# Dilated sliding attention and a two-layer network: q and k turned on VectorE in 32x32 squares, scores summed over two halves of d, loads cut and ordered anew

## The chip, the cores and the metric

The kernel runs on one NeuronCore of one Trainium2 chip. Five engines work on it side by side, each through its own instructions in their order: TensorE (PE in the profile; its weight loads are PEld), VectorE (DVE), ScalarE (ACT), GpSimd (POOL) and SyncE (SP). Transfers between memory and the core's SBUF are issued here by POOL (all loads, which also turn f32 into f16 on the way) and by SP (all stores). The metric is device time in microseconds, from the first instruction to the last of one execution and what lies around it. Three runs of the kernel before gave 331.77, 331.92 and 332.44 us.

## The reference

The inputs q, k and v are 8 batches x 8 heads x 576 positions x 64 (d), all f32. Heads 0 to 3 are plain, heads 4 to 7 are strided.

```
scores = q @ k.T / 8
plain:   key j counts for query i where 0 <= i - j < 32
strided: key j counts for query i where 0 <= i - j < 128 and (i - j) % 4 == 0
attn   = softmax over the keys that count
x      = attn @ v, heads side by side: 4608 tokens x 512
out    = silu(x @ w_in) @ w_out        w_in 512 x 2048, w_out 2048 x 512
```

## The kernel before, in words

**Attention.** In the code `z` is 0 for plain and 1 for strided heads, `b` is the batch. The 576 positions of a plain head are 18 blocks of 32 queries (`QB`), and a block sees 64 keys (`KB`): its own 32 and the 32 ahead. A strided head falls into four classes of 144 positions (position modulo 4), each of which is a plain problem of five blocks, the last half empty. Four heads lie at once on the 128 partitions of a score tile, 32 queries each.

For q and k, d has to lie on the partitions. `load_qk` (line 88) brings several positions of two heads to a partition, as f16, into a tile `n` of the pool `nat` (two buffers). `transpose` (199) turns them on PE against an identity matrix into PSUM tiles `t` of the pool `ps` (four buffers, one bank each), and VectorE and ScalarE copy those into `qT`, `kT` (plain) and `qC`, `kC` (strided), half each (`copies`). `score` (257) and `score_class` (269) are one matmul each for a head and a block: 64 rows (d), 32 columns (queries), 64 keys. `scores` (334) issues 72 of them for a batch's plain heads and 80 for its strided ones, and then on VectorE scales and masks them (`masked`, 288) and takes the maxima (`reduce_max`). `exps` (380) runs on ScalarE, a block at a time with a sum, or, where `shift` (370) has subtracted the maximum on VectorE, in one instruction. `normal` (398) divides on VectorE, and `turned` (413) turns the result, f16, in squares of 32x32 with VectorE's own transpose. `values` (456) multiplies with v on PE, and `finish` (472) casts the result into `xT` on VectorE: the plain heads side by side (478), the strided ones with each element four positions on (480).

**The two layers.** `layer1` (513) runs 16 steps `f`, each eight matmuls of 128x128 weights and 288 tokens into a tile of the pool `big` (two buffers of two banks) and one silu on ScalarE into `gT`. `layer2` (566) serves two batches in nine tiles of 128 tokens, four behind the even and five behind the odd batch: 16 matmuls of 512 columns into a buffer of `big`, a copy `ob` on VectorE, a store. Batch 0 is cut into tokens 0 to 255 and 256 to 575, so that its first layer can start on the first part (`layer1_part`, 530), and its four output tiles are summed side by side (`layer2_first`, 546).

**Order.** The order on each engine is the order in which the program issues its work. From batch 0 on, `plan_of` (601) gives the attention of later batches its place: `plan(s)` issues what is set for step `s`, steps 0 to 15 ahead of the `f` of layer one and steps 16 on ahead of every fourth matmul of layer two. In batch 0, steps -16 to -1 belong to its first part. `later` places `normal`, `turned`, `values` and `finish` of a softmax. Each engine waits at an instruction until its inputs and its buffer are ready, and what is queued behind it waits too. The loads all stand on POOL, in the order of lines 156 to 170, 690 to 700 and the plan.

Of the kernel before, what the change touches and what calls it, by code (L numbers as in the profile page):

```python
# [14 lines left out]
P = 128  # L15
W = 32
# [5 lines left out]
HF = P // 2  # L22
UR = 4
URS = (9, 12)
# [3 lines left out]
def kernel(  # L28
# [13 lines left out]
    HP = H // 2  # L42
    HH = H // 2
# [3 lines left out]
    NM = NB // 2  # L47
    CL = S // DIL
    UPS = [S // u for u in URS]
# [3 lines left out]
    PA = SA // UR  # L53
    PB = (S - SA) // UR
# [16 lines left out]
    ident = cpool.tile([P, P], F16, name="ident")  # L71
# [7 lines left out]

    kTs = [cpool.tile([P, HP // 2, W + S], F16, name=f"kT{i}") for i in range(2)]  # L80
    qTs = [cpool.tile([P, HP // 2, S], F16, name=f"qT{i}") for i in range(2)]
    kCs = [cpool.tile([P, HH, 2, W + CL + TL], F16, name=f"kC{i}") for i in range(2)]
    qCs = [cpool.tile([P, HH, 2, CL + TL], F16, name=f"qC{i}") for i in range(2)]

    NC = CL // W + 1
    vws = [cpool.tile([P, NB + NC * DIL, D], F16, name=f"vw{i}") for i in range(2)]

    def load_qk(b):

        for which in (0, 1):  # L90
            t = nat.tile([P, 2 * sum(URS), D], F16, tag=f"n{which}", name=f"n{which}_{b}")
            u0, u1 = 2 * URS[0], 2 * (URS[0] + URS[1])
            qk[b, 0, which] = t[:, 0:u0].rearrange("p (h u) d -> p h u d", h=2)
            qk[b, 1, which] = t[:, u0:u1].rearrange("p (h u) d -> p h u d", h=2)
        for z in (1, 0) if b == 1 else (0, 1):
            for which, src in ((1, k), (0, q)):
                for i in (0, 1):
                    h = 2 * (2 * z + i)
                    nc.gpsimd.dma_start(  # L99
                        out=qk[b, z, which][i * HF : i * HF + UPS[z]].rearrange("p h u d -> p h (u d)"),  # L100
                        in_=src[b, h : h + 2].rearrange("h (p u) d -> p h (u d)", u=URS[z]),
                    )

    def load_qk0(part, kinds):

        t0, n = ((0, PA), (SA, PB))[part]
        if part not in qk0:
            tiles = [nat.tile([P, 2 * sum(URS), D], F16, tag=f"n{w}", name=f"n{w}_0{part}") for w in (0, 1)]
            qk0[part] = [t[:, 0 : H * UR].rearrange("p (h u) d -> p h u d", h=H) for t in tiles]
        for h in kinds:  # L110
# [6 lines left out]
    def load_v(b, strided=(0, NC), plain=(0, NB)):  # L117
# [12 lines left out]
        for h in range(HH if plain[0] < plain[1] else 0):  # L130
# [3 lines left out]
            )  # L134

    qk = {}
    qk0 = {}
    FC = DFF // 4

    def load_w_in(c):  # L140
# [550 lines left out]
    for c in (1, 2, 3):  # L691
        load_w_in(c)
# [70 lines left out]
```

## Time and profile before

| | |
|---|---|
| median of three runs | 331.92 us (331.77 to 332.44) |
| the profiled execution | 332.05 us, of which 330.3 us are its span |
| mean granted clock of TensorE | 0.984 |
| PE busy | 304.7 us, 92% of the span |
| VectorE busy | 199.3 us, 60% |
| ScalarE busy | 212.5 us, 64% |
| GpSimd busy | 104.3 us, 32% |
| matmuls of layers one and two (lines 518, 537, 578, 554) | 116.4, 20.1, 114.6 and 15.7 us busy |
| transposes of q and k on PE (215, 243, 251) | 11.5, 2.6 and 2.5 us busy |
| loads of k and q in batches 1 to 7 | 56 issues of 144 KB, 5.7 and 6.0 us to landing |
| loads of v | 100 issues of 8 to 72 KB |

A group of the profile names the line, the engine, the operation and the tiles (output before the arrow, inputs behind it), how often it ran, the busy time, and the mean time of one. Matmuls overlap in the array, so that their mean times are longer than the time from one start to the next. The chain that ended last is a list of pieces of work, each released by the one before it; it shows where time was spent that nothing else could cover. The windows give the busy time of each engine within a stretch of the span, with the clock that TensorE was granted.

### The profile page before, as it was taken

The page shows a single profiled execution, that of the slowest core. Times are in us where ns is not written, and L with a number is a line of the kernel's source. Part 1 is how long each engine was busy: PE and PEld are TensorE (multiplying, and loading weights), DVE is VectorE, ACT ScalarE, POOL GpSimd, SP SyncE. Part 2 cuts the span into 40 slices and gives each one's busy share as a digit, 9 for nine tenths or more (in the row PEclk, how much of TensorE's full clock was granted, in tenths as well). Part 3 has the DMA queues.
Part 4 walks back from the last instruction along what each step waited for, and adds up shares of the span by engine and source line. Part 5 has one row for each costly group of instructions (what it writes and reads, how often), then busy time and mean ns, then how long its engine had stood idle before and what let it go on. Part 6 is the DMA issues. An engine that isn't in the chain of part 4 may idle for free.

```text
span 330.3 us, 11556 instructions
## 1 busy us (share of the span) xinstructions
PE 304.7 (92%) x5032; PEld 195.1 (59%) x5032; DVE 199.3 (60%) x369; ACT 212.5 (64%) x703; POOL 104.3 (32%) x178
## 2 busy tenths in 40 slices
PE   3476999479999999999999999999999999999995
PEld 2445764147754577547764577457754677467644
DVE  5578289761679975587558555787558534550011
ACT  2675673306599866997599556996699466916300
POOL 8583728759600291039101940043000000000000
PEclk9997999979999999999999999999999999999999
DMA  6999999999942298029702990049002100110022
GB/s 82 134 101 203 197 192 90 188 220 82 99 78 77 58 127 122 34 69 130 119 4 79 123 175 6 34 79 94 4 20 79 65 2 2 66 64 2 2 83 76
DMA packets 56098, 28.58 MB, mean 87 GB/s; under 512 B 34032, under 2 KB 51568, under 8 KB 56048
## 3 DMA queue, kind: packets, MB, share of 16 engines
q0 software_dynamic: 50720, 18.41, 46.9%
q1 hardware_dynamic: 5328, 9.44, 7.9%
q8 instruction: 39, 0.64, 0.8%
q14 instruction: 11, 0.09, 0.1%
HBM read 36.70 MB, written 9.44 MB: 140 GB/s over the span
## 4 chain that ended last, share of the span: by engine, by line
PE 76%; DVE 9%; ACT 7%; DMA 4%; issue 2%; POOL 1%; POOLq 0%; DVEq 0%; ACTq 0%
PE h L518 34%; PE o L578 29%; ACT pe L393 4%; PE h L537 3%; PE x L446 3%; PE t L215 3%; DMA n<-in_q_dram 3%; DVE pn L409 2%; DMA out_dram<-ob 2%; DVE pt L421 2%; PE s L273 1%; DVE ms L290 1%; DVE nm L328 1%; PE s L261 1%; DVE ob L563 1%
## 5 line engine op out<-in xcount | busy, mean ns | idle before, releaser
L526 ACT ACTIVATE gT<-h 128x576 f16<-128x576 f32 x112 | 72.8, 650 | 70.8 <-PE h L518 70.0
L518 PE MATMUL h<-xT,w_in 128*128 128x288 f16 x896 | 116.4, 288 | 1.9 <-DVE xT L478 1.9
L578 PE MATMUL o<-w_out,gT 128*128 128x512 f16 (+1 forms) x528 | 114.6, 373 | 0.0
L518 PEld LDWEIGHTS <-w_in 128*128 128x128 f16 x896 | 86.4, 98 | 26.4 <-issue 2.5
L393 ACT ACTIVATE pe<-ms,nm 128x64 f32<-128x64 f32 x256 | 85.0, 334 | 5.7 <-DVE nm L328 5.6
L578 PEld LDWEIGHTS <-gT 128*128 128x128 f16 x528 | 50.2, 98 | 54.5
L563 DVE COPY ob<-o 128x512 f32<-128x512 f32 (+1 forms) x37 | 24.7, 669 | 46.4 <-PE o L578 44.0
L121 POOL DMA_DIRECT2D vw<-in_v_dram x32 | 22.0, 693 | 93.4 <-PE x L446 91.2
L393 ACT ACTIVATION_READ_ACCUMULATOR pe<-ms,nm 128x1 f32 x256 | 48.1, 188 | 0.0
L290 DVE SCALAR_TENSOR_TENSOR ms<-s,mask 128x512 f32<-128x512 f32 (+2 forms) x33 | 22.3, 680 | 41.5 <-PE s L273 23.7
L421 DVE STREAM_TRANSPOSE pt<-pn 128x640 f16<-128x640 f16 (+2 forms) x32 | 26.0, 812 | 1.1
L409 DVE TENSOR_TENSOR pn<-pe,r 128x640 f16<-128x640 f32 (+2 forms) x32 | 25.3, 792 | 1.1
L328 DVE TENSOR_REDUCE nm<-ms 128x10 f32<-128x640 f32 (+2 forms) x32 | 25.2, 786 | 1.1
L131 POOL DMA_DIRECT2D vw<-in_v_dram x36 | 23.4, 663 | 4.6 <-DMA vw<-in_v_dram 3.0
L537 PE MATMUL h<-xT,w_in 128*128 128x256 f16 (+1 forms) x128 | 20.1, 318 | 4.0 <-ACT gT L544 3.5
L554 PE MATMUL o<-w_out,gT 128*128 128x512 f16 x64 | 15.7, 399 | 4.3 <-DVE ob L563 4.3
L480 DVE CAST xT<-x 128x288 f16<-128x288 f32 x28 | 19.0, 824 | 0.0
L537 PEld LDWEIGHTS <-w_in 128*128 128x128 f16 x128 | 13.5, 108 | 9.3 <-DMA w_in<-in_moe_w_in_dram 3.8
L126 POOL DMA_DIRECT2D vw<-in_v_dram x32 | 15.9, 513 | 9.3 <-DMA w_out<-in_moe_w_out_dram 7.9
L99 POOL DMA_DIRECT2D n<-in_q_dram x28 | 16.5, 612 | 5.8 <-DMA w_in<-in_moe_w_in_dram 4.0
L99 POOL DMA_DIRECT2D n<-in_k_dram x28 | 16.8, 618 | 4.7 <-PE t L215 2.4
L446 PEld LDWEIGHTS <-vw 32*64 32x64 f16 (+1 forms) x1264 | 13.3, 110 | 7.9 <-issue 7.9
(62 smaller groups left out, 214.6 us busy)
## 6 DMA issues: line engine op xcount, KB each, us to landing
out_dram<-ob SPq DMA_DIRECT2D x35, 256.0 KB, 2.0
n<-in_k_dram POOLq DMA_DIRECT2D x28, 144.0 KB, 5.7
n<-in_q_dram POOLq DMA_DIRECT2D x28, 144.0 KB, 6.0
vw<-in_v_dram POOLq DMA_DIRECT2D x32, 64.0 KB, 4.4
w_in<-in_moe_w_in_dram POOLq DMA_DIRECT2D x4, 512.0 KB, 7.2
w_out<-in_moe_w_out_dram POOLq DMA_DIRECT2D x4, 512.0 KB, 10.1
vw<-in_v_dram POOLq DMA_DIRECT2D x28, 72.0 KB, 3.2
vw<-in_v_dram POOLq DMA_DIRECT2D x32, 8.0 KB, 3.5
```

Source lines behind the costliest of these rows:

```text
L99: nc.gpsimd.dma_start(out=qk[b, z, which][i * HF : i * HF + UPS[z]].rearrange("p h u d -> p h (u d)"), in_=src[b, h : h + 2].rearrange("h ...
L131: nc.gpsimd.dma_start(out=vw[h * QB : h * QB + QB, plain[0] : plain[1]], in_=v[b, h, plain[0] * QB : plain[1] * QB].rearrange("(m p) d -> ...
L290: nc.vector.scalar_tensor_tensor(out=out, in0=in0, scalar=scale, in1=in1, op0=ALU.mult, op1=ALU.add)
L328: nc.vector.tensor_reduce(out=nm[:, 0:w], in_=ms[:, 0:w], axis=AX.X, op=ALU.max, negate=True)
L393: nc.scalar.activation(pe[:, t, :], ms[:, t, :], AF.Exp, bias=nm[:, t : t + 1], accum_out=l[:, t : t + 1],)
L409: nc.vector.tensor_tensor(pn[:, 0:w], a["pe", z, hi][:, 0:w], r[:, 0:w, None].broadcast_to([P, w, KB]), ALU.mult)
L421: nc.vector.transpose(a["pt"][key][:, o : o + w].rearrange("p t c -> p (t c)"), a["pn", z, hi][:, 0:w].rearrange("p t c -> p (t c)"),)
L518: nc.tensor.matmul(h[:, half, 0:HS], w_in16[:, c, f * P : f * P + P], xT[:, c, half * HS : half * HS + HS], start=(c == 0), stop=(c == MC ...
L526: nc.scalar.activation(gT[:, f, s0 : s0 + S].rearrange("p (a c) -> p a c", a=2), h[:, :, 0:HS], AF.Silu)
L537: nc.tensor.matmul(h[:, i, 0 : c1 - c0], w_in16[:, c, (f + i) * P : (f + i + 1) * P], xT[:, c, c0:c1], start=(c == 0), stop=(c == MC - 1),)
L563: nc.vector.tensor_copy(ob, o)
L578: nc.tensor.matmul(o[:, 0, 0:m], gT[:, f, t * P : (t + 1) * P], w_out16[:, f, cols], start=(f == 0), stop=(f == NFF - 1),)
```

## The change

q and k are no longer transposed on PE. `load_rows` brings four heads at once to the 128 partitions, 32 partitions for a head, with 18 positions on a partition for plain heads, and for strided heads in a piece of 16 positions on a partition (the first 512) and one of 4 (the last 128, so that positions 448 to 511 are in both): the tables `PIECES`, `P0` and `P1` hold, for each piece, its column in the tile, the positions on a partition and the first position. `turn_rows` turns such a piece with VectorE's 32x32 transpose straight into `qT`, `kT`, `qC` or `kC`; a square is 32 partitions by 32 of d, so that d now lies on 32 partitions in two halves (`ND` is 2), and each head has a quarter of the partitions. The output of one square is written 18 elements apart for the plain heads (8 and 10 in batch 0), four apart for the strided piece of 16 (two in batch 0), and side by side for the piece of 4. `score` issues two matmuls of 32 rows for a head and a block, one for each half of d, and sums them in PSUM; `opened` holds which bank and head have been started. The last five blocks of the strided classes share one tile (`s[2]`).

The loads of v for the strided tail are one instead of four. Batch 0 needs one `n` tile instead of two. The loads of batch 0 get a new order, with `w_in` and `w_out` and batch 1's q, k and v in it; the masks are copied on ScalarE; ScalarE's first softmax no longer stands behind copies of the second part. `layer1_part` takes four `f` at once in the first part, and `rest_of_part` puts the second part's plain scores, shift and exps behind its first block. The plan gets new steps.

```diff
-    kTs = [cpool.tile([P, HP // 2, W + S], F16, name=f"kT{i}") for i in range(2)]
-    qTs = [cpool.tile([P, HP // 2, S], F16, name=f"qT{i}") for i in range(2)]
-    kCs = [cpool.tile([P, HH, 2, W + CL + TL], F16, name=f"kC{i}") for i in range(2)]
-    qCs = [cpool.tile([P, HH, 2, CL + TL], F16, name=f"qC{i}") for i in range(2)]
+    kTs = [cpool.tile([P, ND, W + S], F16, name=f"kT{i}") for i in range(2)]
+    qTs = [cpool.tile([P, ND, S], F16, name=f"qT{i}") for i in range(2)]
+    kCs = [cpool.tile([P, DIL * ND, W + CL + TL], F16, name=f"kC{i}") for i in range(2)]
+    qCs = [cpool.tile([P, DIL * ND, CL + TL], F16, name=f"qC{i}") for i in range(2)]
...
+    def rows(b):
+
+        if b not in qk:
+            qk[b] = [nat.tile([P, UP + US + UT, D], F16, tag=f"n{w}", name=f"n{w}_{b}") for w in (0, 1)]
+        return qk[b]
+
+    def load_rows(b, z, which, c, u, t0):
+
+        h = HH * z
+        nc.gpsimd.dma_start(
+            out=rows(b)[which][:, c : c + u].rearrange("p u d -> p (u d)"),
+            in_=(q, k)[which][b, h : h + HH, t0 : t0 + QB * u].rearrange("h (p u) d -> h p (u d)", u=u),
+        )
+
     def load_qk(b):
...
+            for which in (1, 0):
+                for c, u, t0 in PIECES[z]:
+                    load_rows(b, z, which, c, u, t0)
+
+    PIECES = [[(0, UP, 0)], [(UP, US, 0), (UP + US, UT, S - QB * UT)]]
+    P0 = [[(0, 8, 0)], [(8, 8, 0)]]
+    P1 = [[(16, 10, SA)], [(26, 8, SA), (34, UT, S - QB * UT)]]
+
+    def load_v(b, strided=(0, NC), plain=(0, NB)):
+
+        vw = vws[b % 2]
+        for m in range(*strided):
+            o = vw[:, NB + m * DIL : NB + m * DIL + DIL].rearrange("p r d -> p (r d)")
+            t0 = m * DIL * QB
+            if t0 + DIL * QB <= S:
                 nc.gpsimd.dma_start(
+                    out=o, in_=v[b, HH:H, t0 : t0 + DIL * QB].rearrange("h (p r) d -> h p (r d)", r=DIL)
                 )
...
+                continue
+            n = HH if b + 1 < B else HH - 1
+            src = bass.AP(v.tensor, (b * H + HH) * S * D + t0 * D, [[S * D, n], [DIL * D, QB], [1, DIL * D]])
+            nc.gpsimd.dma_start(out=o[0 : n * QB], in_=src)
+            if n < HH:
+                nc.gpsimd.dma_start(
+                    out=o[n * QB : n * QB + TL], in_=v[b, H - 1, t0:S].rearrange("(p r) d -> p (r d)", r=DIL)
+                )
...
-    load_qk0(0, (STRIDED,))
-    make_identity(nc, ident)
+    for which in (1, 0):
+        load_rows(0, 1, which, *P0[1][0])
...
-    load_qk0(0, (PLAIN,))
-    load_qk0(1, (slice(0, H),))
+    for which in (1, 0):
+        load_rows(0, 0, which, *P0[0][0])
+    for which in (1, 0):
+        load_rows(0, 1, which, *P1[1][0])
     load_v(0, (0, 2), (0, 8))
     load_w_in(0)
+    for which in (1, 0):
+        load_rows(0, 1, which, *P1[1][1])
+    for which in (1, 0):
+        load_rows(0, 0, which, *P1[0][0])
+    load_w_in(1)
+    load_w_in(2)
+    load_v(0, (2, NC), (8, NB))
+    load_w_in(3)
+    load_qk(1)
+    for c in range(4):
+        load_w_out(c)
+    load_v(1)
...
+    nc.vector.memset(mask[:, 0:3:2, 0:W], NEG)
     for n in (1, 2, 3):
-        nc.vector.tensor_copy(band[n * W : n * W + W], band[0:W])
-    nc.vector.tensor_copy(mask, band[:, None, :].broadcast_to([P, 10, KB]))
-    nc.vector.memset(mask[:, 0:3:2, 0:W], NEG)
+        nc.scalar.copy(band[n * W : n * W + W], band[0:W])
+    nc.scalar.copy(mask[:, 3:10], band[:, None, :].broadcast_to([P, 7, KB]))
+    nc.scalar.copy(mask[:, 0:3:2, W:KB], band[:, None, W:KB].broadcast_to([P, 2, KB - W]))
+    nc.scalar.copy(mask[:, 1], band)
...
+    def turn_rows(b, z, which, c, u, t0):
+
+        a = att(b)
+        src = rows(b)[which][:, c : c + u]
+        if z:
+            dst, t = a[("qC", "kC")[which]], t0 // DIL + W * which
+            nc.vector.transpose(
+                dst[:, :, t : t + QB * u // DIL].rearrange("p x (r e) -> p e x r", r=QB),
+                src.rearrange("p (e r) (a d) -> p e (r a) d", r=DIL, a=ND),
+            )
+        else:
+            dst, t = a[("qT", "kT")[which]], t0 + W * which
+            nc.vector.transpose(
+                dst[:, :, t : t + QB * u].rearrange("p a (r u) -> p u a r", r=QB),
+                src.rearrange("p u (a d) -> p u a d", a=ND),
+            )
+
+    def turn_qk(b, z, pieces=None):
+
+        for which in (1, 0):
+            for piece in pieces or PIECES[z]:
+                turn_rows(b, z, which, *piece)
+
+    def score(b, z, cj, dst, opened):
+
+        a = att(b)
+        c, j = cj
+        at = j * QB
+        for d in range(ND):
+            qs = a["qC"][:, c * ND + d] if z else a["qT"][:, d]
+            ks = a["kC"][:, c * ND + d] if z else a["kT"][:, d]
+            for h in range(HH):
+                r = slice(h * QB, h * QB + QB)
+                key, o = dst
+                nc.tensor.matmul(
+                    o[r],
+                    qs[r, at : at + QB],
+                    ks[r, at : at + KB],
+                    start=(key, h) not in opened,
+                    stop=True,
+                    skip_group_check=True,
                 )
...
+                opened.add((key, h))
...
+    def scores0(z, part, between=lambda: None):
...
             for j in range(8 + 2 * part):
...
+                score(0, 0, (0, 8 * part + j), (j // 8, sd[:, j // 8, j % 8]), opened)
+        between()
...
-    def layer1_part(f, part):
+    def layer1_part(f, part, between=lambda: None):
 
         xT = state[0]["xT"]
         c0, c1 = ((0, SA), (SA, S))[part]
-        h = big.tile([P, 2, 512], F32, tag="big", name=f"h_0_{f}_{part}")
-        for i in (0, 1):
+        n, w = ((4, SA), (2, 512))[part]
+        h = big.tile([P, n, w], F32, tag="big", name=f"h_0_{f}_{part}")
+        for i in range(n):
             for c in range(MC):
...
-        nc.scalar.activation(gT[:, f : f + 2, c0:c1], h[:, :, 0 : c1 - c0], AF.Silu)
+        between()
+        nc.scalar.activation(gT[:, f : f + n, c0:c1], h[:, :, 0 : c1 - c0], AF.Silu)
...
-            for z, s in ((1, -16), (0, -14)):
+            for z, s in ((1, -12), (0, -11)):
                 at(s, normal, 0, z, 1)
                 at(s, turned, 0, z, 1)
-            at(-8, values0, 1, 1)
-            at(-8, finish0, 1, 1)
-            at(-4, values0, 0, 1)
-            at(-4, finish0, 0, 1)
-            transposes(at, 1, 1, 2)
+            at(-4, values0, 1, 1)
+            at(-4, finish0, 1, 1)
+            at(0, values0, 0, 1)
+            at(0, finish0, 0, 1)
+            at(1, turn_qk, 1, 1)
             at(8, scores, 1, 1)
             for hi in (0, 1):
                 at(8, shift, 1, 1, hi)
-            transposes(at, 1, 0, 17)
-            at(20, scores, 1, 0)
-            at(20, shift, 1, 0, 1)
+            at(8, turn_qk, 1, 0)
+            at(14, scores, 1, 0)
+            at(14, shift, 1, 0, 1)
             at(15, load_qk, 3)
             at(15, load_v, 2)
             all_exps(1, 1)
             for hi in (0, 1):
                 at(20, exps, 1, 0, hi)
-            later(at, 1, 1, (18, 19, 24, 31))
-            later(at, 1, 0, (24, 25, 28, 32))
+            later(at, 1, 1, (18, 19, 24, 25))
+            later(at, 1, 0, (22, 23, 28, 29))
         elif b == 1:
             at(16, load_v, 3)
-            transposes(at, 2, 0, 3)
-            transposes(at, 2, 1, 10)
-            transposes(at, 3, 0, 17, (dve, dve))
+            at(3, turn_qk, 2, 0)
+            at(6, turn_qk, 2, 1)
+            at(17, turn_qk, 3, 0)
             at(8, scores, 2, 0)
             at(17, load_qk, 4)
...
-                    for n in (0, 1):
-                        at(1 + 2 * n, transpose, 3, 1, 1 - n, both)
+                    at(1, turn_qk, 3, 1)
                 later(at, b + 1, 0, (0, 0, 4, 6))
...
-                transposes(at, b + 2, 0, 13)
+                at(13, turn_qk, b + 2, 0)
...
-                transposes(at, b + 2, 1, 31)
+                at(31, turn_qk, b + 2, 1)
...
-    transposes0(0, 1, (act, dve))
-    scores0(1, 0)
-    transposes0(0, 0, (act, dve))
+    turn_qk(0, 1, P0[1])
+    scores0(1, 0, lambda: turn_qk(0, 0, P0[0]))
+    scores0(0, 0)
     exps(0, 1, 0)
-    scores0(0, 0)
-    shift(0, 0, 0)
-    load_v(0, (2, NC), (8, NB))
-    for c in (1, 2, 3):
-        load_w_in(c)
-    load_qk(1)
-    for c in range(4):
-        load_w_out(c)
-    transposes0(1, 1, (act, act))
     exps(0, 0, 0)
-    transposes0(1, 0, (act, act))
-    load_v(1)
-    load_qk(2)
+    turn_qk(0, 1, P1[1])
     normal(0, 1, 0)
     turned(0, 1, 0)
     normal(0, 0, 0)
     turned(0, 0, 0)
+    values0(1, 0)
+    finish0(1, 0, (act, act))
     scores0(1, 1)
-    scores0(0, 1)
-    shift(0, 0, 1)
+    turn_qk(0, 0, P1[0])
+    load_qk(2)
     values0(0, 0)
     finish0(0, 0, (act, act))
-    values0(1, 0)
-    finish0(1, 0, (act, act))
     exps(0, 1, 1)
-    exps(0, 0, 1)
+
+    def rest_of_part():
+
+        scores0(0, 1)
+        shift(0, 0, 1)
+        exps(0, 0, 1)
 
     for b in range(B):
         plan = plan_of(b)
         if b == 0:
             for part in (0, 1):
-                for f in range(0, NFF, 2):
-                    plan(f - NFF * (1 - part))
-                    plan(f - NFF * (1 - part) + 1)
-                    layer1_part(f, part)
+                n = 2 if part else 4
+                for f in range(0, NFF, n):
+                    for i in range(n):
+                        plan(f + i - NFF * (1 - part))
+                    layer1_part(f, part, *[rest_of_part] * (f == 0 and part == 0))
```

## The prediction, before the changed kernel was run

> **What bounds the kernel now.** I read the page's shares and slices first, then the chain, then windows and the timelines of single engines. The page's shares and two of its slice rows (busy tenths, 40 slices of 8.26 us):
>
> ```profile
> PE 304.7 (92%) x5032; PEld 195.1 (59%) x5032; DVE 199.3 (60%) x369; ACT 212.5 (64%) x703; POOL 104.3 (32%) x178
> PE   3476999479999999999999999999999999999995
> DVE  5578289761679975587558555787558534550011
> ```
>
> PE is full from 72 us on; its 25.6 idle us lie nearly all in batch 0. So behind 72 us a PE instruction saved or added counts whole, and so does any wait that opens in PE. The chain through batch 4 (start, us, what) prices the two things that the change exchanges:
>
> ```profile
> 199.08 0.61 PE s L273 x64
> 199.69 0.13 PE ss L273 x16
> 199.82 3.05 PE h L518 x24
> 202.87 0.76 PE t L215 x72
> 203.63 3.05 PE h L518 x24
> ...
> 207.54 0.63 PE s L261 x64
> 208.16 0.08 PE ss L261 x8
> ...
> 217.85 0.81 PE x L446 x79
> ...
> 221.35 0.70 PE t L215 x48
> ```
>
> The transposes of one batch (t) take 0.76 + 0.70 us, its scores (s, ss) 0.74 + 0.71 us for 80 and 72 matmuls. VectorE's timeline around the second t, and the rows by shape, price what VectorE does:
>
> ```profile
> 194.73 1.55 DVE L478 CAST xT<-x 128x288 f16<-128x288 f32 x4 [1.78 <-PE x L446]
> ...
> 218.49 2.72 DVE L480 CAST xT<-x 128x288 f16<-128x288 f32 x4
> 221.79 0.76 DVE L228 COPY kC<-t 128x576 f16<-128x576 f16 x1 [0.58 <-PE t L215]
> ...
> 223.13 0.68 DVE L563 COPY ob<-o 128x512 f32<-128x512 f32 x1
> ```
> ```profile
> L421 DVE STREAM_TRANSPOSE pt<-pn 128x640 f16<-128x640 f16 x22 | 18.6, 845 | 0.8
> L421 DVE STREAM_TRANSPOSE pt<-pn 128x512 f16<-128x512 f16 x9 | 6.4, 711 | 0.3
> ```
>
> A transpose costs 1.05 ns per element ((845-711)/128) and about 0.1 us between starts, where its output lies side by side. L478 and L480 cast the same 288 elements; L478 writes them side by side, L480 each 8 bytes on. Four take 1.55 and 2.72 us, a last one 448 and 824 ns; so one follows another after 0.367 and 0.633 us: 0.93 ns more per element, one cycle more by the 1.05 ns.
>
> Batch 0's windows (PE, PEld, DVE, ACT, POOL busy, clock, DMA):
>
> ```profile
> 0.00:30.00 30.00, 15.49 (x341) 11.19 (x342) 19.99 (x47) 17.78 (x63) 21.10 (x40) 0.95 1.01 122
> 60.00:72.00 12.00, 5.44 (x166) 2.91 (x166) 9.89 (x19) 0.78 (x1) 8.14 (x14) 0.83 1.17 217
> ```
>
> In 60 to 72 us VectorE is the limit: the four output tiles of batch 0 wait behind the softmax of batch 1.
>
> **PE's part.** The transposes go: 0.76 + 0.70 us, and by the starts of the records a further 0.10 at each change of operation, 1.66 us per batch. Scores double: 152 more matmuls of 32x64 by 32 rows. Late in a block the records start 8 to 9 ns apart, so 152 x 8.4 ns = 1.28 us. Bounds: 3.4 ns, the start of a block (0.5 us), and 27 ns, one matmul of 64 columns with no neighbour beside it (123 ns for 288 columns at L518). I take 8.4, since blocks with other tiles agree: values (32-row tiles) 0.81 us for 80. Per batch 1.28 - 1.66 = -0.38, for batches 2 to 7 **-2.3 us**. Little is won on PE, because halving d gives back what the transposes took.
>
> [...]
>
> **VectorE's part.** Out go four copies per batch (0.76 us, 0.68 apart: 2.9 us) with ACT's four. In come, for q and for k, a turn of 1152 elements (plain heads, output 36 bytes apart), one of 1024 (strided heads, 8 bytes) and one of 256 (side by side). At 1.05 ns these follow one another after 1.30, 1.17 and 0.37 us; with L480's 0.93 ns more, 2.37, 2.12 and 0.37. Lower bound: the 1.05; upper: a second extra cycle at 36 bytes (3.44). I take L480's, the only row with f16 written apart: a pair costs 4.74 us plain, 4.98 strided, against 1.4 for the copies. VectorE has room for the sum (48 of 73 us busy in batches 4 and 5); what counts is who stands behind the turns.
>
> **Place 1, step 13, batches 2 to 5.** In the times of batch 4: scores at step 10 now take till 200.44, the four maskings and two maxima 3.4 us, till 203.8; the plain turns behind them end at 208.6. PE comes to the scores of step 17 at 207.2 and waits 1.4; four times: **5.6 us**.
>
> **Place 2, step 31.** The casts of L480 end at 221.2; the strided turns then run to 226.2, and only behind them comes ob of the fourth output tile, till 226.9. PE has done that tile by 222.1, does one h till 223.04 in the other buffer of `big` and needs this one: 3.85 us, in batches 2 and 4. Batches 3 and 5 have a fifth tile of 3.46 us in between: ob lands 261.7, PE is at 260.36: 1.35. Sum **10.4 us**. Also behind the turns: normal and turned of the next plain heads, which PE wants 5.9 us later, so free.
>
> **Place 3, batch 1.** The turns of steps 3 and 6 push the maskings of step 8 to 88.2, and the scores of step 13 (PE there at 86.6) need their `ps` tiles: 1.6. The turn of step 17 ends 1.6 after PE reaches step 20. **3.2 us**.
>
> **Place 4, batch 0.** No copy of ACT waits for a load any more ahead of the first softmax (now exps of L387 start at 15.17, behind one). But `turn_qk(0, 1, P1[1])` stands on VectorE ahead of both `normal`, and its last 128 rows are loaded behind w_in(0). Today w_in(0) is there for h at 19.7; 384 KB less stand ahead of it, 3.1 us at the window's 122 GB/s, and POOL's wait of 2.66 us ahead of L141 may go: 14 to 16, the rows by 16 (a choice at the late end, since v's small rows stay ahead), the turns 17.9, two normals and turns of p 1.75 each: first h at about 22.9, 3.2 later than now. The next h needs its buffer back from gT, which now waits for `rest_of_part`: scores, masking and shift, exps, table load 1.28, till about 33; part 0 ends at 39.7 (now 35.5). Then values at step 0 and their casts 1.4; eight steps at 0.545; strided turns 0.6 late; scores 1.4; step 14 reached at 50.8 but masking, shift and plain turns run on VectorE till 57.0; scores 1.3, h 1.1, layer two and values 15.5: 74.9. On VectorE from 58.3: masking and shift 3.8, four normals 9.9, casts and the four ob: 78.1, when batch 1's h can start. Today 24 of its matmuls have run by 76.29, at full pace (2.94 us) a start at 73.35. **+4.7 us**, my roughest term: from -6 (its waits vanish) to +9.
>
> At nothing: the loads (33 fewer issues on POOL at 0.65 us, hidden: POOL is at 32%; exposed, up to the 3.8 us for which L537 now waits for w_in); the masks moved to ACT, idle till 5.5 us (about 2 us there, else ahead of the first masking); ACT's copies, 0.64 us each, beside PE; gT by four f's (8 of 0.60 become 4 of 1.03). load_qk(2) now waits on POOL for the turns of batch 0; only loads of later batches queue there, with 40 us of slack.
>
> **Sum.** -2.3 + 5.6 + 10.4 + 3.2 + 4.7 = +21.6 us. The profiled execution took 332.05 us (span 330.3 and 1.75 around it), 0.13 over the median of 331.92: 332.05 + 21.6 = 353.7, less 0.13: **353.5**. Places 1 and 2 may differ by a fifth each, place 4 by 5: 343 to 362 for this case.
>
> **Rivals.** *Turns at 1.05 ns throughout* (the turned p shows it; against it L480): place 1 closes (206.4 before 207.2), place 2 keeps 2 x 1.95, place 3 none, place 4 +1.4; -2.3 + 3.9 + 1.4 = +3.0: 335.
>
> *Faster: the backlog of 60 to 72 us dissolves.* Turns at 1.05 ns, and scores of batch 1 at step 14 instead of 20 get its softmax done before layer two ends. PE's 6.6 idle us there and 2.1 of slow clock (24 h take 5.03 for 2.94) return: -2.3 + 3.9 - 8.7 = -7.1: 325. It decides if the first ob of batch 0 follows its last matmul within about 1 us. For it: only VectorE held those tiles; against: my tally has VectorE busy there to the end.
>
> *36 bytes cost a second extra cycle*: +2.1 us per plain pair, at step 13 four times, in batch 1 twice, at the start once: 353.5 + 15 = 368.
>
> *Only the 36 byte turns slow*: strided ones at 1.05: -2.3 + 5.6 + 3.9 + 1.6 + 3.5 = +12.3: 344. [...]
>
> *Four row groups take turns at one bank*: 304 matmuls x 27 ns = 8.2 us per batch for 1.45: +6.75 - 1.66, with eight batches some +40, part of it in place of the waits: 375. [...]
>
> **Chances.** Forecast 0.47; turns at 1.05 0.18; backlog gone 0.16; only 36 bytes 0.08; second cycle 0.07; turns at the bank 0.04. The range 326 to 363 leaves out the last two and half of the backlog case: 0.19. Within 0.2% (about what a measurement can tell) lies 0.03 of the 335 case and 0.04 of it below; so faster 0.16 + 0.04 = 0.20, same 0.03, slower 0.77.
>
> **What the profile of the changed kernel would show.** Turns of 1152 elements of about 2.5 us (1.4 if unslowed) and of 1024 at 2.25 (1.25); scores of a batch 1.3 us longer and no t; PE waits before scores at steps 17 and 20 ended by a turn, and before h, ended by ob, after the fourth tile of batches 2 and 4; h of batch 1 starting at 78 instead of 72. Wrong I am if turns show 1.3 us, or if waits of PE behind 78 us stay under 5 us in sum.

## The result, and the profile after

The changed kernel takes **414.61 us** in the median (413.45 to 415.82, four runs) against 332.18 us of the kernel before beside it: ratio 1.247, 95% interval 1.241 to 1.253. The forecast was slower, at 353.5 us with a range of 326 to 363; the direction held, the size did not. The profiled execution took 413.47 us with a span of 411.3.

The page of the changed kernel: shares, slices of 10.3 us, and the chain's shares by engine.

```profile
PE 319.4 (78%) x5312; PEld 202.9 (49%) x5312; DVE 295.9 (72%) x381; ACT 198.1 (48%) x682; POOL 91.0 (22%) x143
PE   0156865977948997695976988588694998999996
DVE  2898798889997999879196893968649597344012
PEclk9996966999897999897896999979699799999999
PE 40%; DVE 38%; issue 11%; DMA 5%; ACT 3%; POOL 2%; POOLq 0%; DVEq 0%; ACTq 0%
```

PE's row, a band of nines before, now has a hole in every batch; VectorE has gained 96.6 us of work (199.3 to 295.9) and carries 38% of the chain; the clock row dips with PE's. The groups of VectorE by shape (busy, mean ns of one) say what the work is, and the view of waits says who stands for it (us in all, times, longest):

```profile
L220 DVE STREAM_TRANSPOSE qT<-n 128x1152 f16<-128x1152 f16 x7 | 37.0, 5279 | 0.0
L220 DVE STREAM_TRANSPOSE kT<-n 128x1152 f16<-128x1152 f16 x7 | 36.0, 5140 | 0.0
L214 DVE STREAM_TRANSPOSE kC<-n 128x1024 f16<-128x1024 f16 x7 | 17.4, 2480 | 0.0
L214 DVE STREAM_TRANSPOSE qC<-n 128x1024 f16<-128x1024 f16 x7 | 16.9, 2408 | 0.0
```
```profile
PE s L242 <- DVE qT L220: 42.3, 9, 6.4
PE h L488 <- DVE ob L535: 12.5, 5, 4.2
PE s L242 <- DVE qC L214: 10.2, 2, 9.4
PE h L488 <- issue: 4.3, 2, 2.9
```

The strided turns (outputs 8 bytes apart) take 2.4 to 2.5 us, close to the 2.25 that was forecast for one. The plain ones (36 bytes apart) take 5.1 to 5.3 where 2.5 was forecast. Around step 13 of batch 4 the timelines of VectorE and PE (start, us) answer to the lines shown of the kernel before:

```profile
258.04 0.82 DVE L299 TENSOR_REDUCE nm<-ms 128x10 f32<-128x640 f32 x1
258.77 5.13 DVE L220 STREAM_TRANSPOSE kT<-n 128x1152 f16<-128x1152 f16 x1
263.56 5.27 DVE L220 STREAM_TRANSPOSE qT<-n 128x1152 f16<-128x1152 f16 x1
```
```profile
261.82 1.03 PE L550 MATMUL o<-w_out,gT 128*128 128x512 f16 x4
268.88 1.90 PE L242 MATMUL s<-kT,qT 32*32 32x64 f16 x128 [6.03 <-DVE qT L220]
```

The pair ends 10.06 us after it began; PE needs its result 4 us after that beginning and stands 6.03 us. Windows over the same wait (PE busy, PEld, DVE, ACT, POOL, then PE's granted clock, DMA share, GB/s) show a second price:

```profile
258.00:262.80 4.80, 4.80 (x37) 3.33 (x35) 4.76 (x3) 3.37 (x6) 0.00 (x0) 1.00 0.00 0
262.80:268.90 6.10, 0.07 (x5) 0.02 (x5) 6.03 (x2) 6.09 (x31) 0.00 (x0) 0.76 0.00 0
268.90:272.90 4.00, 4.00 (x149) 2.66 (x150) 2.86 (x5) 3.24 (x21) 0.00 (x0) 0.51 0.02 4
272.90:277.00 4.10, 4.10 (x20) 1.86 (x19) 2.39 (x6) 4.10 (x26) 0.00 (x0) 1.00 0.18 68
```

Behind the wait TensorE works 4 us at a granted clock of 0.51. So a wait of 6 us costs about 8 (6.0, and half of the 4.0 behind it).

**Where the 81 us of span went.** Batch 1's first h starts at 90.07 us instead of 71.25: **18.8** lie ahead of it. Behind it 321.3 us run instead of 259.0, **62.2** more. Summed over PE's records there, each counted from the end of the one before it: idle times over 0.3 us 48.7 instead of 1.4 (**+47.2**); the layers' matmuls 237.9 instead of 226.4 at the lower clock (**+11.5**); scores 21.5 where transposes and scores took 17.7 (+3.8, slow clock included). The idle time, from the gaps of PE: step 17 (in batch 1 step 20) 6.39, 3.26, 4.69, 6.03, 6.05; behind the fourth output tile 4.19, 1.74, 4.19, 1.72; scores at step 8 of batch 1 2.98; 6.4 in waits that the profile calls "issue", which no engine and no transfer of the program ended.

### The profile page after: what moved, and what is told of

The parts are those of the page before. It is cut to its first block, busy times and chain, and to the rows that moved or that the text cites. A ratio compares the mean times of both kernels' runs of the same rounds, so it can differ in the third digit from the quotient of the medians.

```text
span 411.3 us, 12078 instructions
## 1 busy us (share of the span) xinstructions
PE 319.4 (78%) x5312; PEld 202.9 (49%) x5312; DVE 295.9 (72%) x381; ACT 198.1 (48%) x682; POOL 91.0 (22%) x143
## 4 chain that ended last, share of the span: by engine, by line
PE 40%; DVE 38%; issue 11%; DMA 5%; ACT 3%; POOL 2%; POOLq 0%; DVEq 0%; ACTq 0%
PE h L488 16%; PE o L550 16%; DVE kT L220 8%; DVE qT L220 8%; DVE qC L214 5%; PE s L242 5%; DVE kC L214 4%; DMA n<-in_k_dram 3%; DVE xT L450 3%; DVE nm L299 2%; DVE ms L261 2%; ACT pe L363 2%; DVE ob L535 2%; PE h L508 1%; PE x L416 1%
## 5 line engine op out<-in xcount | busy, mean ns | idle before, releaser
L550 PE MATMUL o<-w_out,gT 128*128 128x512 f16 (+1 forms) x528 | 120.7, 388 | 0.0
L488 PEld LDWEIGHTS <-w_in 128*128 128x128 f16 x896 | 89.3, 101 | 45.4 <-issue 18.8
L114 POOL DMA_DIRECT2D vw<-in_v_dram x32 | 21.4, 676 | 133.4 <-PE x L416 133.0
L242 PE MATMUL s<-kT,qT 32*32 32x64 f16 x1040 | 15.0, 232 | 42.3 <-DVE qT L220 42.3
L220 DVE STREAM_TRANSPOSE qT<-n 128x1152 f16<-128x1152 f16 (+2 forms) x9 | 42.8, 4754 | 0.0
L220 DVE STREAM_TRANSPOSE kT<-n 128x1152 f16<-128x1152 f16 (+2 forms) x9 | 41.5, 4606 | 0.5 <-DMA n<-in_k_dram 0.5
L242 PEld LDWEIGHTS <-qT 32*32 32x32 f16 x1152 | 15.1, 121 | 46.0 <-DVE qT L220 46.0
L214 DVE STREAM_TRANSPOSE kC<-n 128x256 f16<-128x256 f16 (+2 forms) x17 | 22.4, 1319 | 6.8 <-DMA n<-in_k_dram 6.6
L126 POOL DMA_DIRECT2D vw<-in_v_dram x36 | 23.4, 657 | 14.9 <-DMA w_out<-in_moe_w_out_dram 5.6
L416 PE MATMUL x<-pt,vw 32*64 32x64 f16 (+2 forms) x1264 | 15.5, 193 | 9.4 <-DVE pt L391 7.0
L214 DVE STREAM_TRANSPOSE qC<-n 128x256 f16<-128x256 f16 (+2 forms) x17 | 21.9, 1286 | 1.0 <-DMA n<-in_q_dram 0.7
## 6 DMA issues: line engine op xcount, KB each, us to landing
w_out<-in_moe_w_out_dram POOLq DMA_DIRECT2D x4, 512.0 KB, 12.3
n<-in_k_dram POOLq DMA_DIRECT2D x7, 256.0 KB, 10.4
```

The lines of the kernel that those rows point to most:

```text
L214: nc.vector.transpose(dst[:, :, t : t + QB * u // DIL].rearrange("p x (r e) -> p e x r", r=QB), src.rearrange("p (e r) (a d) -> p e (r a) ...
L220: nc.vector.transpose(dst[:, :, t : t + QB * u].rearrange("p a (r u) -> p u a r", r=QB), src.rearrange("p u (a d) -> p u a d", a=ND),)
L242: nc.tensor.matmul(o[r], qs[r, at : at + QB], ks[r, at : at + KB], start=(key, h) not in opened, stop=True, skip_group_check=True,)
L488: nc.tensor.matmul(h[:, half, 0:HS], w_in16[:, c, f * P : f * P + P], xT[:, c, half * HS : half * HS + HS], start=(c == 0), stop=(c == MC ...
L550: nc.tensor.matmul(o[:, 0, 0:m], gT[:, f, t * P : (t + 1) * P], w_out16[:, f, cols], start=(f == 0), stop=(f == NFF - 1),)
```

## The experiments

Two theories of the turns were set against each other first. A: the price goes with the distance at which the output is written, so 5.2 us is what 36 bytes cost. B: a turn has one price per element here and something else in the kernel (the new loads, doubled scores) makes it long.

**side: squares side by side.** In batches 1 to 7 the loads put positions so that a square's 32 columns lie next to each other, one load for each head (shown for the plain heads; the strided ones likewise by class); batch 0 stays.

```diff
+        x, o = (q, k)[which], rows(b)[which]
+        if b > 0:
+            for i in range(HH):
+                r = o[i * QB : i * QB + QB, c : c + u]
+                y = x[b, h + i, t0 : t0 + QB * u]
...
+                    nc.gpsimd.dma_start(out=r, in_=y.rearrange("(m p) d -> p m d", p=QB))
...
-                dst[:, :, t : t + QB * u].rearrange("p a (r u) -> p u a r", r=QB),
...
+                nc.vector.transpose(o.rearrange("p a (u r) -> p u a r", r=QB), i)
```

> The changed kernel with q and k of batches 1 to 7 loaded in another order of positions (one load per head), so that every turn writes its squares side by side; batch 0 is left as it is. Theory A (the turns' price is set by how far apart they write, and the waits of PE come from it): turns of 1152, 1024 and 256 elements take 1.4, 1.25 and 0.45 us for 5.2, 2.45 and 0.45; PE's waits for qT (42 us in sum) fall to those of batch 0 (8 us) and of step 14, its waits for ob (12.5 us) below 4, and the time falls from 414 to 345 to 358 us. Theory B (the bound is the scores with four row groups, or VectorE's share of work as such, or loads): the turns may get shorter, but the time stays above 385.

Measured: **351.60 us** (351.35 to 351.84), ratio 1.059 (1.046 to 1.072): 63 of the 82 us are gone. The same groups of this kernel:

```profile
L246 DVE STREAM_TRANSPOSE kT<-n 128x1152 f16<-128x1152 f16 x7 | 9.6, 1369 | 0.0
L246 DVE STREAM_TRANSPOSE qT<-n 128x1152 f16<-128x1152 f16 x7 | 9.3, 1335 | 0.0
L238 DVE STREAM_TRANSPOSE kC<-n 128x1024 f16<-128x1024 f16 x7 | 8.7, 1236 | 0.0
```

Same elements, same scores, same engine; 1.37 us for 5.14. The waits of PE go with it (in all, times, longest); the first row, 42.3 us in the changed kernel, now lies in batch 0:

```profile
PE s L267 <- DVE qT L248: 7.9, 2, 4.3
PE h L513 <- DVE ob L560: 3.6, 2, 1.8
```

PE's mean clock is 0.974 again, after 0.917 with the change and 0.984 before it, and the layers' matmuls behind batch 1's first h take 225.7 us against 226.4 before: the 11.5 us of slow clock were the waits' doing.

**plain: only the plain heads side by side**; the strided ones stay 8 bytes apart (`side = b > 0 and z == 0`).

> As the run side, but only the plain heads of batches 1 to 7 are turned side by side; the strided heads write 8 bytes apart as in the change; all loads of batches 1 to 7 are one per head. If the price of a write is set by the 16-byte stretches touched, the plain turns hold 3.75 us of the 4.95 us per turn pair and side that the writes cost too much, so most of the gain of side is here: 352 to 368 us. If the price were the same for 8 and 36 bytes (my prediction's), the two kinds would share the gain about evenly, some 380.

Measured: **364.15 us** (one execution). Distance at the strided heads costs 364.15 - 351.60 = 12.6 us; 8.6 of them are waits of h for ob, which are 12.2 us in `plain` and 3.6 in `side`.

**perhead: the changed kernel with one load for each head** in batches 1 to 7, positions as in the change.

> The changed kernel with one load per head instead of one for four heads in batches 1 to 7; all else as in the change, writes apart too. If the time behind batch 0 is set by the turns alone: 414 us within 3. If the shape of the loads (many packets of 4 bytes; 5.4 to 10.4 us to landing) held the turns up, it falls by 5 us or more.

Measured: **414.08 us** (one execution), the time of the changed kernel, though the loads land in 2.0 to 3.5 us instead of 5.4 to 10.4. So neither the loads' form nor their number holds the later batches up, and the plain heads' distance costs 414.08 - 364.15 = 49.9 us.

**price: the operation by itself.** To the end of the kernel before, where its tiles are no longer read, were added turns of 512 elements with outputs 1, 2, 3, 4, 6, 8, 9, 16 and 18 elements apart, casts at 1, 2, 4, 8 and 18, and turns that read apart. Its 361.81 us say nothing but that the tail is longer.

```diff
+    nc.vector.transpose(apart(1), squares())
+    nc.vector.transpose(apart(2), squares())
...
+    nc.vector.transpose(apart(18), squares())
+    nc.vector.tensor_copy(apart(1), mf[:, 0:512].rearrange("p (q r) -> p q r", r=32))
```

> The kernel before with single instructions behind its end: transposes of 512 f16 elements written 1, 2, 3, 4, 6, 8, 9, 16 and 18 elements apart, casts from f32 to f16 of 512 elements written 1, 2, 4, 8, 18 apart on VectorE and on ScalarE, and transposes that read 4, 8, 18 apart. Theory A (a price for each stretch of 16 bytes touched): ns per element on VectorE 1.05, 1.05, 1.6, 2.1, 3.1, 4.2, 4.2, 4.2, 4.2, the casts alike, ScalarE with its own cycle (0.83, 0.83, 1.7, 3.3, 3.3). Theory B (a price for each write that doesn't follow on the last): from 2 or 4 elements on all the same. Theory C (the transpose has a price of its own): the casts stay at 2.1 for 8 and 18 elements. Reads apart cost nothing more by all of them.

The timeline of its end (L746 to L754 are the turns in that order, L755 to L759 VectorE's casts):

```profile
327.56 0.65 DVE L746 STREAM_TRANSPOSE gT<-w_in 128x512 f16<-128x512 f16 x1
328.32 0.75 DVE L747 STREAM_TRANSPOSE gT<-w_in 128x512 f16<-128x512 f16 x1
329.10 1.03 DVE L748 STREAM_TRANSPOSE gT<-w_in 128x512 f16<-128x512 f16 x1
330.23 1.31 DVE L749 STREAM_TRANSPOSE gT<-w_in 128x512 f16<-128x512 f16 x1
331.65 1.88 DVE L750 STREAM_TRANSPOSE gT<-w_in 128x512 f16<-128x512 f16 x1
333.63 2.44 DVE L751 STREAM_TRANSPOSE gT<-w_in 128x512 f16<-128x512 f16 x1
...
341.04 2.37 DVE L754 STREAM_TRANSPOSE gT<-w_in 128x512 f16<-128x512 f16 x1
343.44 0.43 DVE L755 CAST gT<-mask 128x512 f16<-128x512 f32 x1
...
345.16 1.30 DVE L758 CAST gT<-mask 128x512 f16<-128x512 f32 x1
346.49 1.26 DVE L759 CAST gT<-mask 128x512 f16<-128x512 f32 x1
```

The time rises in a line from 4 bytes (0.75) to 16 bytes (2.44) and is flat beyond (2.31 to 2.41 at 18 to 36 bytes). One rule, an estimate from these times, fits all nine within 8%: 0.1 us, and 4.6 ns for each 16-byte stretch that the output enters (512 x 4.6 = 2.36 at 16 bytes and more, half at 8, three eighths at 6), but at least 1.05 ns per element. It also gives the changed kernel's turns: 512 stretches for 1024 elements 8 bytes apart, 2.46 us (2.41 and 2.48 measured), and 1152 for the plain ones, 5.4 us (5.14 and 5.28). So for the turns theory A holds. These casts pay half of that, 1.30 us or 2.4 ns a stretch, so that theory C is right in that a turn is dearer than such a cast. But half is no rule for every cast: these read SBUF, while L480's casts in the kernel before, which read PSUM, follow one another after 0.633 us for 144 stretches (288 elements 8 bytes apart), 4.4 ns each. What makes that difference no run here tests. That two elements share a 16-byte stretch does not make a turn cheap: with two to a stretch (8 bytes apart) it takes 1.31 us instead of 0.65, and with two to three (6 bytes apart) still 1.03. Parts of the expectation failed: "the casts alike" on VectorE, as said; ScalarE's casts took 2.45 us at 16 bytes, 4.8 ns per element where 3.3 was expected; and turns that read 16 and 36 bytes apart took 1.07 and 1.08 us, not 0.65, so reading apart is not free either.

What is left of the 81 us of span are 19.8 in `side`: 12.3 ahead of batch 1's first h (83.55 against 71.25) and 7.5 behind it: waits of h for ob 3.6, "issue" 6.5 instead of 0.6, and matmuls 1.5 less. The next runs take these apart.

**steps: the strided turn out of ob's way.** From `side`; only its step changes, to step 1 of the following batch.

```diff
-                if b == 2:
-                    at(1, turn_qk, 3, 1)
+                at(1, turn_qk, b + 1, 1)
...
-            if b + 2 < B:
-                at(31, turn_qk, b + 2, 1)
```

> The kernel with the squares side by side in batches 1 to 7 (351.6 us), and the strided turn taken from step 31 of layer 2 to step 1 of the next batch's layer 1, behind the normalising of that step. Theory (the two waits of h for ob, 1.8 us each, come from the turn that lies ahead of the ob copy on VectorE): both go, 351.6 - 3.6 = 348.0, range 347 to 349.5, and no h waits for ob. Rival (the copy is late for another reason, or the wait only moves to the scores of step 10): 351 to 353, with a wait of about the same size in the trace.

Measured: **348.36 us** (347.74 to 350.99), ratio 1.058 (1.052 to 1.063), and no h waits for ob in layer one of batches 2 to 7. So the waits came from the turn's place ahead of ob. That the time fits as well, 348.4 for 348.0, is in part luck: in the two profiles, 6.0 us go behind batch 1's first h (3.6 of these waits, 1.6 of "issue" and 1.9 of the layers' matmuls, against a new wait of 1.1 for ob in batch 1), and 2.0 come on ahead of it (85.56 for 83.55), where the two programs are the same. Two microseconds in batch 0 are thus the difference that two executions of one program can show.

**split: the score blocks in quarters.** From `steps`; batch 3's plain scores are in halves, and where the steps are full the last quarter comes up to two steps later. The waits called "issue" stand within or just behind score blocks of 288 or 320 PE instructions (a weight load and a matmul for each product) in about 1.4 us. Counted from 0 over the records of PE and its sequencer, they precede the records 1473, 3009, 4545, 5825, 7105 and 8385 of the changed kernel: each 193 past a multiple of 256. The kernel before has one such wait, 0.63 us within a block of transposes, ahead of record 3009; so four row groups are not needed for it. The page's instruction queue (`q8 instruction: 41, 0.67`) moves 0.67 MB in 41 pieces, 16 KB each; in the changed kernel the trace has one start within the wait of 52.17 to 55.80 (at 53.46) and within that of 158.73 to 161.60 (at 159.03), and one end just ahead of two others. So the author's theory is that TensorE runs out of fetched instructions; the trace does not show what it has fetched. One such wait in `steps`:

```profile
214.24 0.24 PE L267 MATMUL ss<-kC,qC 32*32 32x64 f16 x7
215.83 0.37 PE L267 MATMUL ss<-kC,qC 32*32 32x64 f16 x25 [1.35 <-issue]
```
```diff
-                at(10, scores, b + 1, 1)
+                at(7, scores_part, b + 1, 1, 0, 4)
+                at(8, scores_part, b + 1, 1, 1, 4)
+                at(9, scores_part, b + 1, 1, 2, 4)
+                at(10, scores, b + 1, 1, 4)
```

> The kernel steps, and in batches 1 to 7 the score matmuls of a half in four quarters, each at a step of its own with layer matmuls between, in place of one block of 288 or 320 PE instructions. Nothing is added or taken away. Theory (TensorE uses up its fetched instructions in a block of short matmuls and waits at the next multiple of 256): the idle times behind the blocks of 2.96, 0.82, 1.59 and 1.16 us go, 348.0 - 6.5 = 341.5, range 340.5 to 343.5; the one in batch 0 (3.98) stays. Rival (the idle times belong to the four row groups or to the place of the instruction in the program, not to how densely the instructions come): 347 to 349, with the gaps as large as before.

Measured: **354.05 us** (353.27 to 354.94): 5.7 slower, so both expected times are wrong. The waits did go: all four behind batch 1's first h (1.12, 0.69, 1.75 and 1.35 us) are absent, and the one in batch 0 fell from 4.70 to 1.85. That is what the theory says of the cause; a block of another length would be a second test and was not run. But the same records show what quarters cost: behind the first h, scores take 20.5 us instead of 17.0 and the layers 227.0 instead of 223.9, 6.6 us for 34 more blocks, 0.2 us for each change to scores and back. Another 2.7 us come on ahead of the first h, where batch 1's scores are in quarters too. And a first quarter set right behind `values` waits for its `ps` tile:

```profile
137.80 0.78 PE L267 MATMUL s<-kC,qC 32*32 32x64 f16 x40 [0.80 <-DVE xT L478]
138.51 1.15 PE L518 MATMUL h<-xT,w_in 128*128 128x288 f16 x8
139.59 0.48 PE L267 MATMUL s<-kC,qC 32*32 32x64 f16 x40
```

The changed kernel's records have 41 places 193 past a multiple of 256. At 35 of them PE shows no such wait over 0.3 us, also within score blocks (records 1217, 5569 and 9665); at the other six, all within or just behind score blocks, it costs 0.4 to 3.6 us. Why the distance is 256 and the waits stand at 193 past it isn't shown.

**b0heads, b0side, b0order: batch 0.** All from `side`, which leaves batch 0 as in the change. `b0heads` loads it one head at a time; `b0side` lays it side by side as well; `b0order` is `b0side` with one line moved on VectorE:

```diff
-    turn_qk(0, 1, P1[1])
     normal(0, 1, 0)
     turned(0, 1, 0)
     normal(0, 0, 0)
     turned(0, 0, 0)
+    turn_qk(0, 1, P1[1])
```

> The kernel with the squares side by side in batches 1 to 7 (351.6 us), and in batch 0 one load for each head in place of one for four, positions and turns as they were. If the late landing of the four-head loads (6.4 us, where a one-head load lands in 3 us) is what holds batch 0 up: the first turn starts at 4 to 5 us in place of 6.7 and the time is 348.5 to 350.5. If the four issues on POOL (0.6 us each in place of 0.7 for all) eat that up: 351 to 354, the first turn near 6 us and the later ones no earlier than now.

Measured: 354.03 us (352.15 to 355.91). The first turn starts at 4.91 instead of 6.71 us, but the last pieces come later (the turn of the last four positions of k starts at 23.65, in `side` at 18.86): four issues on POOL stand for one.

> As the one before, with batch 0's positions laid out side by side as well, so that its plain turns write next to each other. Those of 512 and 640 elements take 2.4 to 3.2 us now and would take 0.75 to 0.95: TensorE's waits for qT in batch 0 (4.3 and 3.5 us) go. Theory: 6 to 8 us under the run with one load for each head, so 342 to 346. Rival (batch 0 is bound by its loads, and the turns lie beside them): within 2 us of that run.

Measured: 351.70 us (350.99 to 352.41), 2.3 under it, not 6 to 8; two executions of `b0heads` alone lie 3.8 apart. The plain turns shrank to 0.71 us, and VectorE then stood 8.16 us for the load of the last four positions, with the probabilities behind it:

```profile
25.15 0.45 DVE L238 STREAM_TRANSPOSE kC<-n 128x256 f16<-128x256 f16 x1 [8.16 <-DMA n<-in_k_dram]
```
```profile
28.55 0.61 PE L441 MATMUL x<-pt,vw 32*64 32x64 f16 x32 [13.69 <-DVE r L401]
```

> The kernel b0side (351.7 us), and in batch 0 the turns of the second strided piece stand behind the normalising and turning of the first part's probabilities on VectorE, not ahead of it. Theory (in batch 0 VectorE stood 8.2 us before the turn of the last four positions, whose load is issued behind v and the weights, and the probabilities and TensorE's 9.4 us wait queued behind it): x comes some 8 us earlier and the time is 343.5, range 342 to 346. Rival (TensorE waits for v or for the weights next, or loses it again at the scores of the second part): 349 to 352.

Measured: 353.70 us (352.81 to 355.27). The theory falls: x comes 9 us earlier (19.54 for 28.55), but PE then waits 6.15 us for the strided scores, whose turn still waits for that load, and 6.8 for w_in. So with loads by the head batch 0 waits for what POOL has issued and landed, and this other place of the turns does not mend it. With the change's own four-head loads (6.4 us to landing against 3.1 before) the first turn waits for its load, and behind it VectorE's queue of plain turns (5 us) and strided ones (3.3) holds back the probabilities, as `side` and the changed kernel show alike:

```profile
7.12 0.75 DVE L214 STREAM_TRANSPOSE kC<-n 128x512 f16<-128x512 f16 x1 [5.46 <-DMA n<-in_k_dram]
8.58 0.74 DVE L214 STREAM_TRANSPOSE qC<-n 128x512 f16<-128x512 f16 x1 [0.71 <-DMA n<-in_q_dram]
9.79 2.44 DVE L220 STREAM_TRANSPOSE kT<-n 128x512 f16<-128x512 f16 x1 [0.47 <-DMA n<-in_k_dram]
11.86 2.63 DVE L220 STREAM_TRANSPOSE qT<-n 128x512 f16<-128x512 f16 x1
```

How its 18.8 us divide between load and queue stays open.

**hybrid1 and hybrid2: the kernel before, with VectorE's turns in batches 2 to 7 alone**, side by side, at the steps of `steps`; scores in one block, or in halves at neighbouring steps.

> The kernel before, with batches 0 and 1 as they are (turned by TensorE) and batches 2 to 7 turned by VectorE in squares side by side, loaded one head at a time, the strided turn at step 1, each half's scores in one block. Off the path are batch 0 and the price of distance. What is left by theory: TensorE does 0.38 us less in each of six batches (-2.3) and waits behind the blocks at the multiples of 256 as in the kernel steps (0.69 + 1.75 + 1.34 = 3.8): 330.5 (the kernel before in the last runs) - 2.3 + 3.8 = 332.0, range 330.5 to 333.5. If VectorE's turns still cost the path something that the earlier runs laid to batch 0: 335 or more. If the waits behind the blocks do not come: 328.2.

> As the one before, with each half's scores in two blocks at neighbouring steps. Theory: a block of 144 to 160 PE instructions is short enough that the waits of 3.8 us go, and each of the twelve more changes between scores and layer matmuls costs TensorE 0.17 us, as in the kernel split (6.5 us for 39): 330.5 - 2.3 + 2.0 = 330.2, range 329 to 331.5, no slower than the one before. If the waits stay: 333 to 335.

Measured: hybrid1 **338.62 us** (335.66 to 341.61), ratio 1.021 (1.015 to 1.027); hybrid2 **333.34 us** (330.94 to 335.10), ratio 1.005 (1.002 to 1.008). The 12.3 us ahead of batch 1's first h are gone with the old batches 0 and 1: it starts at 69.81 and 70.06. Behind it both missed upward, hybrid1 into the range that was set for turns that still cost the path something (335 or more), hybrid2 into that for waits that stay (333 to 335). In neither profile does PE wait for a turn of q or k behind batch 1's first h. hybrid1's waits behind blocks are 7.8 us, not 3.8. They precede the records 2497, 3265, 4289, 5569 and 7361, again each 193 past a multiple of 256:

```profile
PE ss L260 <- issue: 7.3, 4, 2.2
```
```profile
97.34 0.30 PE L260 MATMUL ss<-kT,qT 32*32 32x64 f16 x14
99.81 0.20 PE L260 MATMUL ss<-kT,qT 32*32 32x64 f16 x2 [2.17 <-issue]
```

In halves they shrink to 3.2 us but do not vanish. And the gain that was to pay for it is small: scores take 17.5 (one block) and 18.2 us (halves) behind the first h, where the kernel before spends 17.7 on scores and transposes. The six times of hybrid1 spread over 1.8%; the profiled one (336.2 us) is among the shortest, and what the longer ones add isn't shown. No version here beats the kernel before.

## Why the prediction was wrong in size

**The step that failed is the price in VectorE's part.** It took L480's cast (8 bytes apart, 0.93 ns more per element) for turns 8 and 36 bytes apart. At 8 bytes that is nearly right: a turn of 1024 elements took 2.41 to 2.48 us against 2.25 forecast. At 36 bytes it is not: a pair takes 10.06 us, not 4.74, and even the upper bound, "a second extra cycle" (3.44 a turn), lies below the 4.79 from one start to the next. The row was not near in distance, since nothing in the trace of before writes f16 more than 8 bytes apart, and a bound "one step further" was no bound. That it fitted at 8 bytes is in part luck: a cast that reads SBUF takes 0.73 us there instead of 0.43 for 512 elements (`price`), 0.59 ns per element more and not 0.93. With 10.06 for 4.74 in the prediction's own working, place 1 would be 4 x (1.4 + 5.3) = 26.8 and place 3 3.2 + 2 x 5.3 = 13.8, and the sum 385 us; with 5.3 for the plain pair at the start, which the rival "second extra cycle" counts too, 391. So the price is most of the miss, and 24 to 29 us are other things. Neither of the prediction's own signs of being wrong showed: both were set for turns or waits smaller than forecast, none for larger ones.

**Place 1**: mechanism right, but four waits of 20.0 us in sum (3.26, 4.69, 6.03, 6.05) for 5.6. **Place 2**: right in size too, 4.19 and 1.74, twice, for 3.85 and 1.35 (11.8 for 10.4), since it rests on the strided turns' price; what `side` leaves of it, 3.6, `steps` takes away. **Place 3**: 2.98 + 6.39 = 9.4 for 3.2, by the price; but the 2.98 stand at step 8, for the plain turn itself, and not, as forecast, at step 13 for `ps` tiles.

**Place 4**: batch 1's h at 90.07, not 78.1. The prediction held the loads at "nothing", or 3.8 us; that four heads in one load of 128 KB land in 6.4 us, where a load of 128 KB landed in 3.1 before, was not in it, nor that PE would stand for 3.63 us in a wait called "issue" behind batch 1's scores. PE's first matmul starts at 9.38 us, 5 later than before. Of the 18.8 us that batch 1's h comes later, 6.5 go in `side`, where batch 0 stays as in the change, so that much, give or take the 2 us by which executions differ there, is again the price, in batch 1's turns.

**PE's part** (-2.3) was too kind: where neither clock nor waits disturb it (`side`, `steps`), scores take 17.0 to 17.1 us against 17.7, so -0.6 to -0.7. The pace of 8.4 ns was right within a block (8.0 to 8.3 at full clock); blocks cost more at their ends.

**Not in the sum at all**: the half clock behind a wait (0.51 for 4 us behind the one of 6.03; +11.5 us in all) and the waits called "issue" (6.4 us for 0.6, +5.8). The first could have been read before: the prediction itself used the clock of 0.83 in the window of 60 to 72 us for batch 0, and did not apply it to the waits that it forecast.

**The rivals.** "Second extra cycle" had the right mechanism, distance, but at 368 was still short. "Only 36 byte turns slow" is refuted by the 2.4 us at 8 bytes and by `plain` (12.6 us). "Turns at 1.05 ns" holds for outputs side by side (`side`: 1.37 us for 1152 elements), not here. "Backlog dissolves" failed with batch 0. "Row groups take turns at a bank", nearest in number at 375, was the author's assumption and is refuted: records in a block with four of them start 8.0 to 8.3 ns apart at full clock and 13 at the slow one, not 27, and `side` has the same blocks.

## What to carry to other kernels

Price a strided write by the number of 16-byte stretches it enters, not by elements: here a turn of 32x32 squares, 512 elements, costs 15% more at 4 bytes (0.75 us for 0.65), double at 8 (1.31) and nearly four times from 16 on (2.31 to 2.44); what a cast pays for a stretch has to be measured, since it was 2.4 ns in one place and 4.4 in another. Loads that lay the positions out for it had no one waiting for them in batches 1 to 7. When a wait on a full TensorE is forecast, add the half-clock time behind it: here 4 us at 0.51 behind a wait of 6.03 us. And moving work off the bound engine pays only by what that engine really gets back, which halving d reduced to 0.1 us a batch.

## What was not expected of the hardware

- A turn's price by output distance: 0.65, 0.75, 1.03, 1.31, 1.88, 2.44 us for 512 elements at 2, 4, 6, 8, 12 and 16 bytes, then 2.31 to 2.41 up to 36; VectorE's cast out of SBUF 0.43 to 1.30.
- TensorE stops for 0.4 to 4.7 us at some records that stand 193 past a multiple of 256, within or just behind dense blocks of short matmuls (0.41 to 3.63 us at six of 41 in the changed kernel, 4.7 the longest in `steps`); with quarters of the block only the one in batch 0 was left (1.85 us), and each change to another kind of matmul and back costs 0.2 us (6.6 us for 34 more blocks).
- After a wait of 6.03 us in the changed kernel, TensorE had 4 us at a granted clock of 0.51.
- Fewer loads are not fewer packets: the change's four-head loads raise the packets from 56,098 to 71,844.
